# Keeping the filter's cosine products in PSUM, where DVE's sums of residue pairs read them

## The chip, the cores and the metric

The kernel runs on one core of a Trainium2 chip. The core's engines work side by side: PE (TensorE) multiplies matrices and leaves its results in PSUM, DVE (VectorE) and ACT (ScalarE) read and write both PSUM and SBUF, POOL (GpSimd) works on SBUF, and SP issues most of the transfers to and from memory. The metric is the time of one execution in microseconds (us).

## The reference

Two parts follow each other. The first multiplies x by a long convolution of x * v with a filter that a small network makes from position embeddings; the second is a feed-forward layer with a rational function in place of an activation.

```python
h_filt = (np.maximum(pos_emb @ w1, 0.0) @ w2) * np.exp(-0.01 * pos)[:, None]
u = x * v
Uf = np.fft.rfft(u, n=2 * S, axis=1)
Hf = np.fft.rfft(h_filt, n=2 * S, axis=0)
y = np.fft.irfft(Uf * Hf[None], n=2 * S, axis=1)[:, :S, :]
attn = x * y                       # (2, 12480, 128)
h = attn.reshape(-1, 128) @ w_in   # d_ff = 2048
g = (a[0] + a[1]*h + a[2]*h**2 + a[3]*h**3) / (1 + abs(b[0])*abs(h) + abs(b[1])*h**2 + 1e-6)
out = g @ w_out
```

## The kernel before

The Fourier transforms are made of matrix products with tables of cosines and sines, in two stages with a twiddle between them. A position is n = 128 * m + t; t is the residue. Stage 1 sums over m, one matmul for each channel (`s1_mm`, `L146`), and leaves K1 = 90 cosine columns and 90 sine columns per channel in a PSUM tile `cs` (two banks, 128 partitions, four channels, so 720 columns in all). The twiddle (`s1_twiddle`, `L164` and `L165`) multiplies them on DVE by a cosine and by a sine, and a complex sum makes `z`. Stage 2 multiplies over the residues on PE.

The filter takes a short cut in stage 2: the residues stand in pairs, and one half of the partitions holds one member, the other half the other. So `s1h_out` makes its sums across the halves, in four instructions of 64 partitions x 360 columns (`L551` to `L554`), which read the two twiddled tiles `ta` and `tb` from SBUF. The complex sums of the data (`s1_out`, `L170` and `L171`) are whole tiles and run on POOL.

The first part's main loop goes over g, from 0 to 34, with groups of four channels (32 groups) in a software pipeline. One iteration issues, in this order: the filter's stage 1 for group g (`L146` with `hf`, then `s1h_out` on DVE); for group g - 1 the filter's stage 2 (`L558`), its copy by ACT (`L594`) and transfer to memory, and the data's stage 1 (`L146` with `hu`, then `L164` and `L165` on DVE with `tw`, then POOL); for group g - 2 the data's stage 2 (`L181` to `L184`) and the product of the spectra (`L196` and `L197` on DVE, `L199` and `L200` on POOL); for group g - 3 the inverse stage (`L565`), ACT's copies (`L572`) and two sums on POOL (`L576`, `L577`). It ends with a piece of u = x * v on DVE (`L234`, for g below 24) or, from g = 24 on, with conversions of the second part's weights while they last.

Each engine works through its instructions in the order of the program. The PSUM tiles `cs` share four places of two banks each, with five tiles to an iteration; a new tile takes a place when the last reader of the tile that had it is done. The tags `ta` and `tb` have two places each in SBUF, which the three users of an iteration (filter, data, product) share.

The second part begins after the loop and works on its own tiles; it computes the second batch's convolution beside the feed-forward layer.

Of the kernel before, what the change touches and what calls it, by code (L numbers as in the profile page):

```python
# [9 lines left out]
F32 = mybir.dt.float32  # L10
# [3 lines left out]
ALU = mybir.AluOpType  # L14
# [6 lines left out]
N2 = 128  # L21
# [8 lines left out]
K1 = (N1 + 1) // 2  # L30
CG = 4
# [69 lines left out]
def build(ctx: ExitStack, tc, x, v, pos_emb, w1, w2, w_in, w_out, moe_a, moe_b,  # L101
          f1_d, tw_d, twh_d, dft_d, dfth_d, idft_d, idfth_d, g_d, win_d, ident_d, out):
    nc = tc.nc
# [45 lines left out]
    def pair(pool):  # L149

        t = pool.tile([N2, 2, 2, 2 * K1], F32, tag="ta", name="ta", bufs=2)
        return t, (t[:, 0], t[:, 1])

    def s1_twiddle(pool, cvt, tw, n):
        if n == 2:
            t, ab = pair(pool)
            src = cvt[:, 0, 0:4 * K1].rearrange("p (i k) -> p i k", i=2)
            nc.vector.tensor_tensor(out=t, in0=src.unsqueeze(1).to_broadcast(t.shape),
                                    in1=tw.unsqueeze(2).to_broadcast(t.shape), op=ALU.mult)
            return ab  # L160
        sh = [N2, n // 2, 2, 2 * K1]
        ta, tb = (pool.tile(sh, F32, tag=t, name=t, bufs=2) for t in ("ta", "tb"))
        src = cvt[:, 0:n // 2, 0:4 * K1].rearrange("p b (i k) -> p b i k", i=2)
        nc.vector.tensor_tensor(out=ta, in0=src, in1=tw[:, 0:1, :].unsqueeze(1).to_broadcast(sh), op=ALU.mult)  # L164
        nc.vector.tensor_tensor(out=tb, in0=src, in1=tw[:, 1:2, :].unsqueeze(1).to_broadcast(sh), op=ALU.mult)  # L165
        return ta.rearrange("p b i k -> p (b i) k"), tb.rearrange("p b i k -> p (b i) k")
# [80 lines left out]
    with ExitStack() as st:  # L247
        sp = st.enter_context(tc.tile_pool(name="sp", bufs=1))
# [4 lines left out]
        twh = sp.tile([N2, 2, 2 * K1], F32, name="twh")  # L253
# [290 lines left out]


        def s1h_out(cvt, z):
            a, bb = s1_twiddle(sp, cvt, twh, CG)
            lo, hi = slice(0, H2), slice(H2, N2)
            re, im = slice(0, K1), slice(K1, 2 * K1)
            E = nc.vector  # L550
            E.tensor_tensor(out=z[lo, 0], in0=a[lo, :, re], in1=bb[hi, :, im], op=ALU.add)  # L551
            E.tensor_tensor(out=z[hi, 0], in0=a[hi, :, im], in1=bb[lo, :, re], op=ALU.subtract)
            E.tensor_tensor(out=z[lo, 1], in0=a[lo, :, im], in1=bb[hi, :, re], op=ALU.subtract)
            E.tensor_tensor(out=z[hi, 1], in0=a[hi, :, re], in1=bb[lo, :, im], op=ALU.add)  # L554

        def s2h_mm(cvt, z):
            for i in range(2):
# [24 lines left out]
        for g in range(NG + 3):  # L582
            a = g
            if a < NG:
                zh[a] = ctile(sp, "zh", 2, CG)
                t = cvs()
                s1_mm(t, hf[a // gq], a % gq * CG, CG, MF)
                s1h_out(t, zh[a])
            a = g - 1
# [10 lines left out]
            a = g - 2  # L600
# [5 lines left out]
            a = g - 3  # L606
# [441 lines left out]
```

## Time and profile before

| | |
|---|---|
| median of 3 runs | 2523.94 us (2522.64 to 2524.48) |
| the profiled execution, its span | 2523.35 us, 2521.5 us |
| DVE, PE, ACT, POOL busy over the span | 2385.3, 2163.8, 2099.0, 544.7 us |

The span runs from the first to the last instruction that the profiler saw; the execution's own time is 1.85 us longer. Busy time says how long an engine had an instruction under way, whether or not this instruction itself made headway. [...]

### The profile page before, as it was taken

What the parts mean: (1) busy time and instruction counts of PE and PEld (TensorE: products, weight loads), DVE (VectorE), ACT (ScalarE), POOL (GpSimd) and SP (SyncE); (2) the same over time, 40 slices, a digit from 0 to 9 for tenths busy, and PEclk for the clock granted to TensorE, in tenths of its full rate; (3) what the DMA queues carried; (4) which work ended last, traced back from release to release, by engine and by line L of the source; (5) the groups of instructions that cost most, each with busy time, mean ns of one, the idle gap of its engine ahead of it and who ended that gap; (6) DMA issues with size and microseconds to landing.
All of it is one profiled execution on the core that took longest, in us unless ns stands there. A gap on an engine that the chain in (4) does not pass through costs nothing.

```text
span 2521.5 us, 33957 instructions
## 1 busy us (share of the span) xinstructions
PE 2163.8 (86%) x13344; PEld 1817.2 (72%) x13344; DVE 2385.3 (95%) x1945; ACT 2099.0 (83%) x1919; POOL 544.7 (22%) x522
## 2 busy tenths in 40 slices
PE   7888878799989998998999879887888898888887
PEld 4666666687777777787887767776776776667766
DVE  8999996999999998999999999999999999999997
ACT  5312212999999997999899999999999999999996
POOL 3466655321432143225222100000000000000000
PEclk8998998899999999999999999999999999999998
DMA  7445414622242133223222121111111111111100
GB/s 142 101 110 114 109 64 118 107 68 50 64 91 72 39 72 80 52 71 72 57 52 56 46 54 40 31 28 42 30 43 32 32 39 43 42 29 37 31 12 12
DMA packets 357825, 150.26 MB, mean 60 GB/s; under 512 B 292518, under 2 KB 339752, under 8 KB 354776
## 3 DMA queue, kind: packets, MB, share of 16 engines
q1 hardware_dynamic: 350632, 124.24, 23.4%
q10 hardware_dynamic: 7024, 23.76, 3.0%
q8 instruction: 107, 1.75, 0.3%
q14 instruction: 62, 0.51, 0.1%
HBM read 99.78 MB, written 48.17 MB: 59 GB/s over the span
## 4 chain that ended last, share of the span: by engine, by line
ACT 35%; DVE 28%; PE 24%; issue 9%; POOL 2%; DMA 1%; SPq 0%; ACTq 0%; DVEq 0%; POOLq 0%
ACT r L902 9%; ACT r L899 9%; ACT q L862 7%; PE acc L930 7%; DVE v L916 7%; ACT v L871 6%; DVE r L912 4%; DVE q L907 3%; PE cv L205 3%; PE cv L206 2%; ACT q L895 2%; DVE ta L192 2%; DVE v L881 2%; PE cs L146 1%; PE cv L146 1%
## 5 line engine op out<-in xcount | busy, mean ns | idle before, releaser
L930 PE MATMUL acc<-wout,v 128*128 128x128 f32 (+2 forms) x6656 | 833.1, 284 | 57.7 <-DVE v L916 33.7
L930 PEld LDWEIGHTS acc<-wout,v 128*128 128x128 f32 (+2 forms) x6656 | 788.7, 192 | 109.9 <-DVE v L916 52.7
L871 ACT ACTIVATE v<-h,sc 128x980 f32<-128x980 f32 (+1 forms) x416 | 640.2, 1539 | 5.5 <-PE acc L930 5.5
L862 ACT ACTIVATE q<-h 128x980 f32<-128x980 f32 (+1 forms) x416 | 582.2, 1458 | 6.6 <-PE h L854 6.6
L881 DVE SCALAR_TENSOR_TENSOR v<-v,sc,h 128x980 f32<-128x980 f32 (+1 forms) x416 | 505.3, 1215 | 64.1 <-ACT v L871 62.3
L895 ACT ACTIVATE q<-q,sc 128x1960 f32<-128x1960 f32 (+1 forms) x208 | 495.6, 2383 | 0.0
L899 ACT ACTIVATE r<-q,sc 128x1960 f32<-128x1960 f32 (+1 forms) x208 | 494.7, 2378 | 0.2 <-DVE v L916 0.2
L902 ACT ACTIVATE r<-r 128x1960 f32<-128x1960 f32 (+1 forms) x208 | 476.5, 2291 | 0.0
L907 DVE SCALAR_TENSOR_TENSOR q<-q,sc,r 128x1960 f32<-128x1960 f32 (+1 forms) x208 | 466.3, 2242 | 4.9 <-ACT r L902 1.1
L916 DVE SCALAR_TENSOR_TENSOR v<-v,sc,r 128x1960 f32<-128x1960 f32 (+1 forms) x208 | 465.4, 2238 | 0.1
L912 DVE SCALAR_TENSOR_TENSOR r<-q,r 128x1960 f32<-128x1960 f32 (+1 forms) x208 | 450.9, 2168 | 0.1
L852 PE MATMUL h<-ahi,win_l 128*128 128x490 f32 (+1 forms) x832 | 365.2, 439 | 99.5 <-DVE v L881 97.3
L853 PE MATMUL h<-alo,win_h 128*128 128x490 f32 (+1 forms) x832 | 321.5, 386 | 0.0
L854 PE MATMUL h<-ahi,win_h 128*128 128x490 f32 (+1 forms) x832 | 319.3, 384 | 0.0
L852 PEld LDWEIGHTS h<-ahi,win_l 128*128 128x128 f32 x832 | 158.9, 191 | 158.7 <-DVE v L881 133.3
L199 POOL TENSOR_TENSOR yy<-ta 128x180 f32<-128x180 f32 x64 | 117.8, 1841 | 367.5 <-DVE ta L192 367.5
L854 PEld LDWEIGHTS h<-ahi,win_h 128*128 128x128 f32 x832 | 159.2, 191 | 26.6
L853 PEld LDWEIGHTS h<-alo,win_h 128*128 128x128 f32 x832 | 159.9, 192 | 15.9 <-DVE alo L823 0.4
L798 PE MATMUL cv<-yc,gt 90*98 90x128 f32 x1004 | 130.8, 277 | 33.4 <-DVE an L804 30.7
L798 PEld LDWEIGHTS cv<-yc,gt 90*98 90x98 f32 x1004 | 114.8, 165 | 53.5 <-DVE an L804 49.7
L209 ACT ACTIVATE ys<-cv 90x512 f32<-90x512 f32 x64 | 76.9, 1202 | 71.3 <-PE cv L206 71.3
L205 PE MATMUL cv<-idft,yy 128*90 128x256 f32 x256 | 79.9, 394 | 61.4 <-DVE ta L192 36.5
(109 smaller groups left out, 2496.1 us busy)
## 6 DMA issues: line engine op xcount, KB each, us to landing
yc<-y_d SPq DMA_DIRECT2D x23, 900.0 KB
gt<-in_g_dram SPq DMA_DIRECT2D x48, 344.5 KB
h_d<-hg ACTq DMA_DIRECT2D x32, 360.0 KB
y_d<-ys ACTq DMA_DIRECT2D x16, 720.0 KB
hg<-h_d SPq DMA_DIRECT2D x64, 180.0 KB
y_d<-ys SPq DMA_DIRECT2D x16, 720.0 KB
xq<-in_x_dram SPq DMA_DIRECT2D x32, 196.0 KB
vq<-in_v_dram SPq DMA_DIRECT2D x32, 196.0 KB
```

The lines of the kernel that those rows point to most:

```text
L852: nc.tensor.matmul(out=t[:, k, 0:w], lhsT=wl, rhs=hi[:, 0:w], start=True, stop=False)
L853: nc.tensor.matmul(out=t[:, k, 0:w], lhsT=wh, rhs=lo[:, 0:w], start=False, stop=False)
L862: nc.scalar.activation(out=halves(st_q[s], i, width(s)), in_=st_h[s, i], func=AF.Abs, **({} if short else {"scale": col("b0")}))
L871: nc.scalar.activation(out=v, in_=st_h[s, i], func=AF.Square, bias=col("s"))
L881: stt(out=v, in0=v, scalar=col("k"), in1=h, op0=ALU.add, op1=ALU.mult)
L895: nc.scalar.activation(out=whole(st_q, s), in_=whole(st_q, s), func=AF.Square, bias=col("dl"))
L899: nc.scalar.activation(out=whole(st_r, s), in_=whole(st_q, s), func=AF.Ln, **({"bias": col("ka")} if short else {}))
L902: nc.scalar.activation(out=whole(st_r, s), in_=whole(st_r, s), func=AF.Exp, scale=-1.0)
L907: nc.vector.scalar_tensor_tensor(out=q, in0=q, scalar=col("ka") if short else 0.0, in1=whole(st_r, s), op0=ALU.add, op1=ALU.mult)
L912: nc.vector.scalar_tensor_tensor(out=r, in0=whole(st_q, s), scalar=2.0, in1=r, op0=ALU.subtract, op1=ALU.mult)
L916: nc.vector.scalar_tensor_tensor(out=v, in0=v, scalar=col("p0" if short else "a0"), in1=whole(st_r, s), op0=ALU.add, op1=ALU.mult)
L930: nc.tensor.matmul(out=acc[j][0:k, q // 128, :], lhsT=g[:, i, q:q + k], rhs=wout[:, f, :], start=(f == 0 and q == 0), stop=(f == NF - 1), ...
```

## The change

`s1h_out` no longer calls `s1_twiddle`. It makes the product with the sines first, to SBUF as before (`bb`, from the tag `tb`). Then it multiplies the PSUM tile by the cosines in place, and the four sums read their first input there. The tile `ta` of the filter is gone. The sums have the same shapes and the same partitions as before; the views have one dimension more, since PSUM's columns lie in two banks.

```diff
         def s1h_out(cvt, z):
-            a, bb = s1_twiddle(sp, cvt, twh, CG)
+            sh = [N2, CG // 2, 2, 2 * K1]
+            bb = sp.tile(sh, F32, tag="tb", name="tb", bufs=2)
+            a = cvt[:, 0:CG // 2, 0:4 * K1].rearrange("p b (i k) -> p b i k", i=2)
+            E = nc.vector
+            E.tensor_tensor(out=bb, in0=a, in1=twh[:, 1:2, :].unsqueeze(1).to_broadcast(sh), op=ALU.mult)
+            E.tensor_tensor(out=a, in0=a, in1=twh[:, 0:1, :].unsqueeze(1).to_broadcast(sh), op=ALU.mult)
+            z = z.rearrange("p r (b i) k -> p r b i k", i=2)
             lo, hi = slice(0, H2), slice(H2, N2)
             re, im = slice(0, K1), slice(K1, 2 * K1)
-            E = nc.vector
-            E.tensor_tensor(out=z[lo, 0], in0=a[lo, :, re], in1=bb[hi, :, im], op=ALU.add)
...
+            E.tensor_tensor(out=z[lo, 0], in0=a[lo, :, :, re], in1=bb[hi, :, :, im], op=ALU.add)
...
```

On DVE, one steady iteration of the loop before, from the filter's products to the data's (each row: line, operation, output and inputs, shape; in brackets the engines whose signals the instruction waits for):

```order
L164 TENSOR_TENSOR ta<-cs,twh 128x720 [waits DVE_49,PE_49,Pool_49]
L165 TENSOR_TENSOR tb<-cs,twh 128x720 [waits DVE_49]
L551 TENSOR_TENSOR zh<-ta,tb 64x360 [waits DVE_49]
L552 TENSOR_TENSOR zh<-ta,tb 64x360
L553 TENSOR_TENSOR zh<-ta,tb 64x360 [waits DVE_49]
L554 TENSOR_TENSOR zh<-ta,tb 64x360 [waits DVE_49]
L164 TENSOR_TENSOR ta<-cs,tw 128x720 [waits PE_49,Pool_49]
L165 TENSOR_TENSOR tb<-cs,tw 128x720
```

And the same place in the changed kernel, whose lines have numbers that are 6 higher from the sums on:

```order
L552 TENSOR_TENSOR tb<-cs,twh 128x720 [waits DVE_49,PE_49,Pool_49]
L553 TENSOR_TENSOR cs<-cs,twh 128x2x360
L557 TENSOR_TENSOR zh<-cs,tb 64x360 [waits DVE_49]
L558 TENSOR_TENSOR zh<-cs,tb 64x360
L559 TENSOR_TENSOR zh<-cs,tb 64x360
L560 TENSOR_TENSOR zh<-cs,tb 64x360
L164 TENSOR_TENSOR ta<-cs,tw 128x720 [waits PE_49]
L165 TENSOR_TENSOR tb<-cs,tw 128x720 [waits Pool_49]
```

No instruction has moved or gone: six are six, in the same place among DVE's others. The product with the cosines now comes second and writes `cs`, the sums read `cs` and `tb`, and the data's wait for POOL has moved from `ta` to `tb`.

On PE the matmuls keep their order, but the place that each `cs` tile takes has changed, and with it what is waited for. Before, from the data's stage 2 in one iteration to the start of the next (`L565` is the inverse stage, `L146` with `hf` the filter's stage 1):

```order
L181 MATMUL cs<-zu,dft 128x360 [waits PE_49,Activation_49,Pool_49]
...
L565 MATMUL cs<-idfth,yy 90x128 [waits DVE_49,PE_49,Pool_49]
L565 MATMUL cs<-idfth,yy 90x128 [waits Pool_49]
L565 MATMUL cs<-idfth,yy 90x128 x6
L146 MATMUL cs<-f_66,hf_93 128x180 [waits Activation_49]
```

In the changed kernel, over two iterations (`L571` is the inverse stage there, `L564` the filter's stage 2):

```order
L571 MATMUL cs<-idfth,yy 90x128 [waits Activation_49,Pool_49]
L571 MATMUL cs<-idfth,yy 90x128 [waits Pool_49]
L571 MATMUL cs<-idfth,yy 90x128 x6
L146 MATMUL cs<-f_66,hf_93 128x180 [waits DVE_49]
...
L564 MATMUL cs<-zh,dfth 128x360 [waits DVE_49,PE_49]
...
L571 MATMUL cs<-idfth,yy 90x128 [waits DVE_49,PE_49,Pool_49]
L571 MATMUL cs<-idfth,yy 90x128 [waits Pool_49]
L571 MATMUL cs<-idfth,yy 90x128 x6
L146 MATMUL cs<-f_66,hf_94 128x180 [waits Activation_49]
```

Before, the inverse stage took the filter's place and waited for DVE's second product, and the next filter's stage 1 waited for ACT. Now the two take turns: in one iteration the next filter's stage 1, in the other the inverse stage, waits for DVE's last sum (`L560`), while the other one waits for ACT's copy.

## Rows read from the trace of the kernel before

**Rows 1.** Busy us by stretch and engine; granted clock, DMA share, GB/s.

```profile
core 0: us, PE busy (x) PEld busy (x) DVE busy (x) ACT busy (x) POOL busy (x), PEclk, DMA share, GB/s
98.00:112.00 14.00, 14.00 (x72) 11.03 (x71) 13.68 (x20) 1.93 (x5) 6.17 (x7) 0.99 0.44 100
112.00:318.00 206.00, 179.71 (x887) 138.50 (x886) 202.81 (x222) 40.39 (x71) 140.76 (x123) 0.93 0.48 109
318.00:367.00 49.00, 37.39 (x172) 28.34 (x171) 48.12 (x66) 8.35 (x16) 26.72 (x28) 0.90 0.21 66
367.00:405.00 38.00, 34.26 (x178) 26.89 (x177) 36.33 (x42) 8.55 (x16) 25.91 (x25) 0.96 0.23 77
```

**Rows 2.** DVE's groups by shape, 60 to 460 us: busy us, mean ns.

```profile
L552 DVE TENSOR_TENSOR zh<-ta,tb 64x360 f32<-64x360 f32 x32 | 40.8, 1276 | 1.0
L551 DVE TENSOR_TENSOR zh<-ta,tb 64x360 f32<-64x360 f32 x32 | 40.8, 1275 | 1.1
...
L553 DVE TENSOR_TENSOR zh<-ta,tb 64x360 f32<-64x360 f32 x32 | 19.8, 619 | 1.0
L554 DVE TENSOR_TENSOR zh<-ta,tb 64x360 f32<-64x360 f32 x32 | 16.9, 527 | 1.0
```

**Rows 3.** Timeline, DVE, one iteration before POOL's long sums begin: start, duration.

```profile
104.04 0.89 DVE L164 TENSOR_TENSOR ta<-cs,twh 128x720 f32<-128x720 f32 x1
...
105.78 0.53 DVE L551 TENSOR_TENSOR zh<-ta,tb 64x360 f32<-64x360 f32 x1
106.34 0.53 DVE L552 TENSOR_TENSOR zh<-ta,tb 64x360 f32<-64x360 f32 x1
...
112.27 0.90 DVE L164 TENSOR_TENSOR ta<-cs,twh 128x720 f32<-128x720 f32 x1
```

**Rows 4.** Timeline, DVE and POOL, in a steady iteration.

```profile
237.31 1.26 POOL L576 TENSOR_TENSOR ys<-qt 90x512 f32<-90x512 f32 x1
...
237.34 1.63 DVE L551 TENSOR_TENSOR zh<-ta,tb 64x360 f32<-64x360 f32 x1
...
238.53 1.57 POOL L577 TENSOR_TENSOR ys<-qt 90x512 f32<-90x512 f32 x1
...
239.00 1.49 DVE L552 TENSOR_TENSOR zh<-ta,tb 64x360 f32<-64x360 f32 x1
...
243.27 0.90 DVE L196 TENSOR_TENSOR pta<-cs,hg 128x720 f32<-128x720 f32 x1
...
244.09 0.90 DVE L197 TENSOR_TENSOR ptb<-cs,hg 128x720 f32<-128x720 f32 x1
244.28 0.82 POOL L171 TENSOR_TENSOR zu<-ta,tb 128x360 f32<-128x360 f32 x1
```

**Rows 5.** Timeline, DVE: first products of iterations 24, 25, 28 and 31.

```profile
317.77 0.90 DVE L164 TENSOR_TENSOR ta<-cs,twh 128x720 f32<-128x720 f32 x1
...
332.92 0.90 DVE L164 TENSOR_TENSOR ta<-cs,twh 128x720 f32<-128x720 f32 x1
...
366.98 0.90 DVE L164 TENSOR_TENSOR ta<-cs,twh 128x720 f32<-128x720 f32 x1
...
395.44 0.91 DVE L164 TENSOR_TENSOR ta<-cs,twh 128x720 f32<-128x720 f32 x1
```

**Rows 6.** Timeline, PE, where it runs without a gap.

```profile
98.84 0.77 PE L181 MATMUL cs<-zu,dft 128*128 128x360 f32 x2
...
104.92 0.77 PE L181 MATMUL cs<-zu,dft 128*128 128x360 f32 x2
...
107.34 1.91 PE L565 MATMUL cs<-idfth,yy 128*90 128x128 f32 x16
109.09 1.39 PE L146 MATMUL cs<-f,hf 82*128 82x180 f32 x8
```

**Rows 7.** Timeline, DVE: reads of PSUM at the second part's start.

```profile
425.57 0.56 DVE L804 TENSOR_TENSOR an<-cv,xt 98x384 f32<-98x384 f32 x1 [4.45 <-PE cv L798]
428.25 0.42 DVE L804 TENSOR_TENSOR an<-cv,xt 98x256 f32<-98x256 f32 x1 [2.12 <-PE cv L798]
```

More of the change, by code (lines that the diff above doesn't have):

```diff
@@ L546, in s1h_out @@
         def s1h_out(cvt, z):
-            a, bb = s1_twiddle(sp, cvt, twh, CG)
+            sh = [N2, CG // 2, 2, 2 * K1]
[5 more added lines that the diff above has]
+            z = z.rearrange("p r (b i) k -> p r b i k", i=2)
             lo, hi = slice(0, H2), slice(H2, N2)
             re, im = slice(0, K1), slice(K1, 2 * K1)
-            E = nc.vector
-            E.tensor_tensor(out=z[lo, 0], in0=a[lo, :, re], in1=bb[hi, :, im], op=ALU.add)
-            E.tensor_tensor(out=z[hi, 0], in0=a[hi, :, im], in1=bb[lo, :, re], op=ALU.subtract)
-            E.tensor_tensor(out=z[lo, 1], in0=a[lo, :, im], in1=bb[hi, :, re], op=ALU.subtract)
-            E.tensor_tensor(out=z[hi, 1], in0=a[hi, :, re], in1=bb[lo, :, im], op=ALU.add)
+            E.tensor_tensor(out=z[lo, 0], in0=a[lo, :, :, re], in1=bb[hi, :, :, im], op=ALU.add)
+            E.tensor_tensor(out=z[hi, 0], in0=a[hi, :, :, im], in1=bb[lo, :, :, re], op=ALU.subtract)
+            E.tensor_tensor(out=z[lo, 1], in0=a[lo, :, :, im], in1=bb[hi, :, :, re], op=ALU.subtract)
+            E.tensor_tensor(out=z[hi, 1], in0=a[hi, :, :, re], in1=bb[lo, :, :, im], op=ALU.add)
         def s2h_mm(cvt, z):
```

## The prediction

> **What bounds the kernel now.** I read the busy times by stretch first [rows 1]. The change touches only the first part's loop over groups of four channels, whose last iteration ends near 405 us of the span. In it DVE is busy 202.81 of the 206 us between 112 and 318, while POOL has 140.76 and ACT 40.39. So DVE sets the pace, and a microsecond taken from DVE there is a microsecond off the end, until another engine is as full. PE, with 179.71, is the next one.
>
> Then I asked which of DVE's instructions cost more than they should. The groups by form show the four sums of `s1h_out`, all of one shape, at means of 1275, 1276, 619 and 527 ns [rows 2]. The timeline tells why. In the iteration that begins at 104.04, where POOL does not run `L576` and `L577` yet, each sum lasts 0.53 us and the next begins 0.56 us after it [rows 3]. In a steady iteration `L551` begins at 237.34, just after POOL's `L576`, ends only after it, and takes 1.63; `L552` falls on `L577` and takes 1.49 [rows 4]. Both inputs of these sums lie in SBUF. The products with one input in PSUM do not suffer: `L197` runs beside POOL's `L171` and keeps 0.90, `L196` before it has the same [rows 4]. So what is lost is mutual exclusion between POOL and a DVE instruction that reads two SBUF tensors: 1.63 + 1.49 - 2 x 0.53 = 2.06 us in an iteration.
>
> The starts of the filter's first product, `L164`, give the periods. There are 20 iterations (g = 4 to 23) from 112.27 to 317.77 [rows 3, 5], 10.275 us each, against 8.23 us from 104.04 to 112.27 [rows 3]. The difference, 2.05, is the loss just found.
>
> **The change, part by part.**
>
> *Products.* One product (with the sines, to SBUF) stays as it is. The other reads and now also writes the same PSUM tile. No row of before shows DVE writing PSUM. Lower end: no extra cost, since DVE reading PSUM costs what reading SBUF does (below). Upper end: every element needs two turns at the bank, so 0.75 us more for 720 elements (0.90 less a fixed part of some 0.15). I take 0, as the rows on reading are the nearest, and keep the upper end as a rival.
>
> *Sums.* Four per iteration, 64 x 360, now with one input in PSUM. From DVE's PSUM reads of 256 and 384 columns, 0.42 and 0.56 us [rows 7], 360 columns come to 0.53, equal to the sum from SBUF in rows 3. The step from one to the next could be shorter than 0.56: `L196` and `L197` start 0.82 apart though each takes 0.90 [rows 4], and in the same way sums would start 0.45 apart. But `L551` and `L552` have no wait between them in the order shown above, and still start 0.56 apart [rows 3]; what keeps them apart looks like the change of partition half, which stays. I take 0.56. With 0.45 the iteration would be 0.33 to 0.44 shorter, of which PE (below) would let some 0.4 through: 8 us over 20 iterations at most.
>
> [...]
>
> *Exclusion.* Gone for the sums. `L234`, which multiplies two SBUF tiles, keeps its own; it is within the 8.23. POOL's work in an iteration starts at the same instructions as before (its order does not change), and its `L577` loses the wait for the sums.
>
> *PE and the PSUM tiles.* The filter's `cs` tile is now held until the last sum, and in the order shown above one iteration's `L571`, and in the next iteration the filter's `L146`, waits for it. What PE must do in an iteration is read where it runs without a gap: 6.08 us from `L181` at 98.84 to `L181` at 104.92 (an iteration without `L565`), and 1.75 for `L565` (107.34 to 109.09): 7.83 [rows 6]. From the iteration's first product, the last sum ends after 1.74 + 3 x 0.56 + 0.53 = 3.95 us. Then `L571` and the next filter `L146` take 1.75 + 1.39 [rows 6]: 7.09, before DVE needs that tile at 8.23. So this wait is covered with 1.1 us. [...]
>
> *The sum.* 20 steady iterations x (10.275 - 8.23) = 40.9. Iteration g = 24 (317.77 to 332.92) has the same two slow sums ahead of weight work that does not change: 2.05. In g = 25 to 27 the exclusion already falls on the weight work and the sums are short: 0. From g = 28 on there is no `L234`: three periods from 366.98 to 395.44 are 9.49 each [rows 5]; DVE alone would come down to 1.74 + 4 x 0.56 + 4 x 0.82 = 7.26, but PE's 7.83 stops it, so I take 7.9: 4 x 1.59 = 6.4. Together 49.3. Off this 2 us, for a few stretches at 1.2 GHz: the mean clock was 0.93 of 2.4 GHz in the steady stretch, but 0.99 from 98 to 112, where PE had no idle time [rows 1], and with PE busy 95% of an iteration I expect the latter. So 47.3 less than the profiled execution's 2523.35 us (span 2521.5), an execution that stands 0.6 under the median of the runs: **2476 us**. As a check, the sums' excess over 0.53 is 40.8 + 40.8 + 19.8 + 16.9 - 128 x 0.53 = 50.5 us [rows 2], the most that DVE can give by this way. The second part is the same, instruction for instruction, and begins that much earlier.
>
> **The rivals.**
>
> *PE becomes the bound.* For it: 7.83 is close under 8.23; at the old mean clock it is 7.83 / 0.93 = 8.42, and with stalls at the new tile wait some 8.6. Against it: the clock in rows 1 where PE was full. Then 20 x 1.675 + 1.7 + 4 x 0.89 = 39 saved: 2484; 2497 if the period is 9.1.
>
> *The product in place runs at half rate.* 0.75 more in each iteration: 20 x 1.3 + 1.3 - 7 x 0.75 + 4 x 1.46 = 27.9 saved: 2495. Nothing in the profile speaks for or against it.
>
> *Sums from PSUM have a larger fixed cost.* Half of the fixed 0.14 us of rows 7 again would be 0.28 an iteration, 28 x 0.28 = 8 us: 2484. Against it: rows 7 and 3 together. [...]
>
> *The change doesn't do what it says.* If POOL also blocks an instruction with one SBUF input, or the lost time moves to `L234`, nothing is gained: 2523. Against it: `L196` and `L197` in rows 4.
>
> *Slower.* PSUM serves DVE at half rate in all five new accesses, the product in place and four reads by half the partitions with a change of half. That is 0.75 + 4 x 0.375 = 2.25 an iteration, above the 2.05 won; it decides from 2.05 on. Steady iterations lose 0.2 each (4 us), and the seven iterations without slow sums lose 2.25 (16): 2543. Against it: rows 7, at full rate, though with 98 partitions from the first on.
>
> **How the numbers follow.** The forecast has 0.60, PE as bound 0.17, the dearer sums 0.06, half rate in the product 0.09, no effect 0.04, slower 0.04. The range from 2470 to 2498 holds the first four and some 2 us of overlap between sums; it leaves out less than 0.2. The likeliest one's own range is 2470 to 2480. Below 0.2% (5 us) a measurement of this kernel can't tell a change from none; the first four cases are faster by more, so faster 0.92, same 0.04, slower 0.04.
>
> **What would show it.** Right: sums at 0.53 beside POOL's two long instructions, the product in place at 0.90, iterations of 8.2 to 8.3 us through the steady stretch, POOL's second long one (`L577`, 1.57 in rows 4) down to the 1.26 of the first, and DVE's first instruction of the second part (425.57 before, rows 7) near 378. Wrong: a product of 1.2 to 1.7; PE without idle time and DVE waiting for `L146` or `L184`, with a granted clock under 0.95 there; sums over 0.6; `L234` longer than before.

## The result

The changed kernel takes 2475.69 us in the median of 4 runs (2473.72 to 2477.18), the kernel before 2523.57 (4 runs, 2522.64 to 2524.48). The ratio of the two is 0.9812, with a 95% interval of 0.9801 to 0.9823 (the runs below give their ratio to the kernel before in the same way). The forecast of 2476 lies 0.3 us from the median. The profiled execution took 2475.52 us, its span is 2473.6 (2521.5 before).

### The profile page after: what moved, and what is told of

Its sections match the earlier page's. It is cut to its first block, busy times and chain, and to the rows that moved or that the text cites. A ratio compares the mean times of both kernels' runs of the same rounds, so it can differ in the third digit from the quotient of the medians.

```text
span 2473.6 us, 33923 instructions
## 1 busy us (share of the span) xinstructions
PE 2129.4 (86%) x13344; PEld 1799.1 (73%) x13344; DVE 2335.8 (94%) x1945; ACT 2098.8 (85%) x1919; POOL 534.7 (22%) x522
## 3 DMA queue, kind: packets, MB, share of 16 engines
q8 instruction: 107, 1.75, 0.3%
## 4 chain that ended last, share of the span: by engine, by line
ACT 35%; DVE 27%; PE 24%; issue 9%; POOL 2%; DMA 1%; SPq 0%; ACTq 0%; DVEq 0%; POOLq 0%
ACT r L908 9%; ACT r L905 9%; ACT q L868 7%; PE acc L936 7%; DVE v L922 7%; ACT v L877 6%; DVE r L918 4%; DVE q L913 4%; PE cv L205 3%; ACT q L901 2%; PE cv L206 2%; DVE ta L192 2%; DVE v L887 2%; PE cs L571 2%; PE cv L146 1%
## 5 line engine op out<-in xcount | busy, mean ns | idle before, releaser
L199 POOL TENSOR_TENSOR yy<-ta 128x180 f32<-128x180 f32 x64 | 119.8, 1871 | 369.5 <-DVE ta L192 369.5
```

## The profile after

First DVE's groups by shape, 60 to 460 us before [rows 2] and 60 to 420 us here, where the first part ends earlier; the columns are busy us and mean ns, then the idle time ahead.

```profile
L553 DVE TENSOR_TENSOR cs<-cs,twh 128x720 f32<-128x720 f32 x32 | 28.8, 900 | 0.0
L552 DVE TENSOR_TENSOR tb<-cs,twh 128x720 f32<-128x720 f32 x32 | 28.6, 894 | 3.9 <-POOL yy L200 2.4 <-POOL zu L171 1.5
L558 DVE TENSOR_TENSOR zh<-cs,tb 64x360 f32<-64x360 f32 x32 | 17.1, 535 | 0.4
...
L557 DVE TENSOR_TENSOR zh<-cs,tb 64x360 f32<-64x360 f32 x32 | 16.8, 525 | 1.1
```

All 128 sums are short now, 525 to 535 ns against means of 1275, 1276, 619 and 527. The product in place (`L553`) takes 900 ns, the one to SBUF 894: writing PSUM costs DVE nothing more here.

The timeline of DVE, POOL and PE in a steady iteration (start, duration, and in brackets a wait), which answers to [rows 4]:

```profile
202.67 0.89 DVE L552 TENSOR_TENSOR tb<-cs,twh 128x720 f32<-128x720 f32 x1
...
203.49 0.89 DVE L553 TENSOR_TENSOR cs<-cs,twh 128x720 f32<-128x720 f32 x1
204.38 1.27 POOL L582 TENSOR_TENSOR ys<-qt 90x512 f32<-90x512 f32 x1
204.41 0.53 DVE L557 TENSOR_TENSOR zh<-cs,tb 64x360 f32<-64x360 f32 x1
204.95 0.54 DVE L558 TENSOR_TENSOR zh<-cs,tb 64x360 f32<-64x360 f32 x1
205.50 0.53 DVE L559 TENSOR_TENSOR zh<-cs,tb 64x360 f32<-64x360 f32 x1
205.61 1.27 POOL L583 TENSOR_TENSOR ys<-qt 90x512 f32<-90x512 f32 x1
206.04 0.54 DVE L560 TENSOR_TENSOR zh<-cs,tb 64x360 f32<-64x360 f32 x1
...
206.72 1.95 PE L571 MATMUL cs<-idfth,yy 128*90 128x128 f32 x16 [0.46 <-DVE zh L560]
...
210.84 0.89 DVE L552 TENSOR_TENSOR tb<-cs,twh 128x720 f32<-128x720 f32 x1
```

The sums now lie side by side with POOL's two long instructions and neither delays the other: `L583` has the 1.27 of `L582`, where the second of the pair took 1.57 [rows 4]. PE does wait for the last sum before `L571`, but DVE has no gap for it: the next iteration begins 8.17 us after this one.

The busy times by stretch (PE, PEld, DVE, ACT, POOL; then the granted clock, which is TensorE's as a share of its full speed; DMA share, GB/s) answer to [rows 1]:

```profile
112.00:276.00 164.00, 157.20 (x872) 126.46 (x871) 161.86 (x221) 39.44 (x70) 134.31 (x123) 1.00 0.58 135
276.00:318.00 42.00, 30.61 (x151) 24.43 (x149) 41.40 (x58) 8.04 (x15) 25.36 (x25) 0.89 0.24 75
```

DVE is still the fullest engine of the loop (99%), PE is at 96%, and the granted clock of the steady stretch is 1.00. The second part begins at DVE's `L810`, 47.40 us earlier than in [rows 7]:

```profile
378.17 0.56 DVE L810 TENSOR_TENSOR an<-cv,xt 98x384 f32<-98x384 f32 x1 [4.45 <-PE cv L804]
```

From the starts of the filter's first product in both traces comes the ledger, with what the prediction gave each stretch:

| stretch | before | after | difference | forecast |
|---|---|---|---|---|
| span's start to g = 4 | 112.27 | 112.56 | +0.29 | 0 |
| g = 4 to 23 | 205.50 | 163.95 | -41.55 | -40.9 |
| g = 24 | 15.15 | 13.06 | -2.09 | -2.05 |
| g = 25 to 27 | 34.06 | 36.37 | +2.31 | 0 |
| g = 28 to 30 | 28.46 | 23.47 | -4.99 | -4.8 |
| g = 31 to the second part | 30.13 | 28.76 | -1.37 | -1.6 |
| second part | 2095.93 | 2095.43 | -0.50 | 0 |
| sum | 2521.5 | 2473.6 | -47.90 | -49.3, with 2 off: -47.3 |

## The experiments

The theory is that POOL's reads of SBUF and DVE's sums with both inputs in SBUF shut each other out, and that the change wins only by taking one input out of SBUF. The rivals are that the new order of the products, the missing tile `ta` or the new places of the PSUM tiles win something themselves, and that POOL's two instructions delay DVE in another way than by their reads.

### The order alone

The kernel before with the products in the new order, both to SBUF, and the sums reading SBUF:

```diff
         def s1h_out(cvt, z):
-            a, bb = s1_twiddle(sp, cvt, twh, CG)
+            tb, ta = (sp.tile(sh, F32, tag=t, name=t, bufs=2) for t in ("tb", "ta"))
...
+            nc.vector.tensor_tensor(out=tb, in0=src, in1=twh[:, 1:2, :].unsqueeze(1).to_broadcast(sh), op=ALU.mult)
+            nc.vector.tensor_tensor(out=ta, in0=src, in1=twh[:, 0:1, :].unsqueeze(1).to_broadcast(sh), op=ALU.mult)
```

> The kernel before with the filter's two products in the new order (sines first, cosines second), both to SBUF, and the four sums from SBUF. Theory (a sum that reads two SBUF tensors is shut out while POOL works): nothing is won, steady iterations of 10.28 us, two sums of an iteration at 1.4 to 1.65 us, 2524 us within 3. Rival (the gain came from the order of the products, the tags' places or the places of the PSUM tiles): 2476 to 2500.

Measured: 2522.91 us, ratio 1.0 (0.999 to 1.0009). The timeline of a steady iteration (start, duration) shows the same slow pair as [rows 4]:

```profile
237.46 1.27 POOL L581 TENSOR_TENSOR ys<-qt 90x512 f32<-90x512 f32 x1
237.49 1.63 DVE L556 TENSOR_TENSOR zh<-ta,tb 64x360 f32<-64x360 f32 x1
238.69 1.56 POOL L582 TENSOR_TENSOR ys<-qt 90x512 f32<-90x512 f32 x1
239.15 1.49 DVE L557 TENSOR_TENSOR zh<-ta,tb 64x360 f32<-64x360 f32 x1
240.67 0.53 DVE L558 TENSOR_TENSOR zh<-ta,tb 64x360 f32<-64x360 f32 x1
```

The order of the products wins nothing by itself. This run keeps the tile `ta`, and its PSUM tile is free after the second product, as before; the next run bears on those.

### POOL only writes

The kernel before, with POOL's two sums of the inverse stage (`L576`, `L577`) replaced by memsets of the same elements (the kernel leaves those two sums out):

```diff
-            engines[0].tensor_tensor(out=dst[:, 1:3], in0=a, in1=b, op=ALU.add)
-            engines[1].tensor_tensor(out=dst[:, 0:4:3], in0=a, in1=b, op=ALU.subtract)
+            for e, o, op in zip(engines, (dst[:, 1:3], dst[:, 0:4:3]), (ALU.add, ALU.subtract)):
+                if e is nc.gpsimd:
+                    e.memset(o, 0.0)
+                else:
+                    e.tensor_tensor(out=o, in0=a, in1=b, op=op)
```

> The kernel before with POOL's two inverse-stage sums of an iteration turned into memsets of the same elements, so that POOL writes them and reads nothing (the inverse sums are left out on POOL; the filter's sums still read two SBUF tensors). Theory, with the loss put down to POOL's reads: the filter's sums fall to 0.53 to 0.6, iterations to 8.2 to 8.35 us, and the time to 2468 to 2480 with less to wait for in the weight iterations as well. Rival (POOL's writing is enough to shut DVE out, or sums from SBUF are slow by themselves): sums of 1 us or more remain, 2500 to 2524.

Measured: 2466.66 us, ratio 0.9776 (0.9761 to 0.9791), 1.3 us below the expected range. The timeline shows DVE's sums, unchanged from before and with both inputs in SBUF, beside POOL's memsets (two in the first line, merged):

```profile
204.37 0.99 POOL L578 MEMSET ys<- 90x512 f32 x2
204.43 0.53 DVE L551 TENSOR_TENSOR zh<-ta,tb 64x360 f32<-64x360 f32 x1
204.99 0.53 DVE L552 TENSOR_TENSOR zh<-ta,tb 64x360 f32<-64x360 f32 x1
205.54 0.53 DVE L553 TENSOR_TENSOR zh<-ta,tb 64x360 f32<-64x360 f32 x1
```

With POOL writing, not reading, `L551` and `L552` take 0.53 again, and 20 iterations (112.30 to 276.65) take 8.22 us each. The two memsets are shorter than the sums they stand for (0.99 us together), but `L551` lies wholly beside them and loses nothing. So there are two ways to the same 8.2: take DVE's second input out of SBUF, or POOL's inputs away. That these sums have two SBUF inputs is harmless alone. This kernel has the old order, the tile `ta` and the old places of the PSUM tiles; as its period is within 0.02 us of the changed kernel's 8.20, those explain none of the 2.05 us that an iteration won. (Of the 9 us by which this run lies below the changed kernel, 5.9 are in iterations 24 to 27, 276.65 to 320.18 here and 276.51 to 325.94 there; the next run is about that stretch. Another 2.6 lie between g = 31 and the second part.)

So a sum of this shape takes 0.53 beside POOL's memsets with both inputs in SBUF, and 0.53 beside POOL's sums with one input in PSUM (`L557` in the changed kernel).

### The weight conversions moved

In the changed kernel, iterations 24 to 26 still take 13.1 us each. In them DVE's conversions of weights stand at the end of the iteration and fall on POOL's instructions. Here they follow right behind `s1h_out`:

```diff
+            weights = not (uw and gq * (uw[0][0] - 1) <= g)
+            if weights:
+                next(wg, None)
             a = g - 1
...
-            if uw and gq * (uw[0][0] - 1) <= g:
+            if not weights:
                 mult_u(nc.vector)
-            else:
-                next(wg, None)
```

> The changed kernel with the weight conversions of iterations 24 to 27 moved from the end of the iteration to right behind the filter's sums, where POOL waits for the data's products. Theory: the conversions run without POOL beside them, 2.3 us in place of 5.8, iterations 24 to 26 go from 13.1 to 9.6 us, and PE's long wait in iteration 27 goes too: 2462 to 2466. Rival (they meet POOL wherever they stand, or PE sets the pace there): 2472 to 2477.

Measured: 2464.95 us, ratio 0.9766 (0.9753 to 0.978). The groups of DVE from 276 to 318 us (busy us, mean ns), first of the changed kernel, then of this one:

```profile
L325 DVE TENSOR_TENSOR i<-i,i 128x256 int32<-128x256 int32 x3 | 4.4, 1483 | 0.0
L323 DVE TENSOR_SCALAR i<-raw 128x256 int32<-128x256 int32 x3 | 4.1, 1355 | 0.0
...
L320 DVE TENSOR_SCALAR i<-raw 128x256 int32<-128x256 int32 x3 | 3.1, 1032 | 0.0
```

```profile
L325 DVE TENSOR_TENSOR i<-i,i 128x256 int32<-128x256 int32 x3 | 1.2, 410 | 0.0
...
L323 DVE TENSOR_SCALAR i<-raw 128x256 int32<-128x256 int32 x3 | 0.8, 282 | 0.0
...
L320 DVE TENSOR_SCALAR i<-raw 128x256 int32<-128x256 int32 x3 | 0.8, 281 | 0.0
```

Where POOL is idle, a conversion takes 0.28 us instead of 1.03 or 1.36. `L320` and `L323` have one input, so one input alone doesn't free an instruction from the exclusion. The iterations g = 24 to 26 come down to 9.83, 9.92 and 9.95, and DVE's first instruction of the second part (378.17 in the changed kernel) to 365.97. Of these 12.2 us the median shows 10.7; the profiled execution, 2466.17 us, is the longest of its five.

The run bears on g = 27 too. With the conversions out of the way, PE's longest wait for the last sum falls. The sums of PE's waits from 100 to 350 us (us, times, longest), in the changed kernel and here:

```profile
PE cs L571 <- DVE zh L560: 19.0, 12, 6.9
```

```profile
PE cs L571 <- DVE zh L560: 10.1, 13, 1.9
```

The granted clock from 276 to 318 us rises from 0.89 to 1.00, and g = 27 takes 8.11 us (306.06 to 314.17) instead of 10.08.

### The product u = x * v moved as well

`L234`, the last DVE instruction with two SBUF inputs in the loop, put to the same place:

```diff
-            weights = not (uw and gq * (uw[0][0] - 1) <= g)
-            if weights:
+            if uw and gq * (uw[0][0] - 1) <= g:
+                mult_u(nc.vector)
+            else:
                 next(wg, None)
...
-            if not weights:
-                mult_u(nc.vector)
```

> As the run with the weight conversions moved, and DVE's piece of u is moved to the same place in the other iterations. Theory: the piece takes 1.04 in place of 1.11 to 1.16 us and POOL is not shut out by it, but the data's products come 0.88 us later and the next iteration's first product then waits for POOL's second complex sum: iterations of 8.1 to 8.3, so 2462 to 2468. Rival (that wait becomes long): 8.5 and more, over 2470.

Measured: 2476.5 us, ratio 0.9819 (0.9805 to 0.9832), 11.5 us more than with the conversions alone. The expectation failed; the rival has the time, but not its reason, for the wait that it names is short (0.15 below). The steady period is 8.755 us (113.35 to 288.44 for g = 4 to 23) against 8.195. The timeline (start, duration, wait):

```profile
202.68 1.27 POOL L582 TENSOR_TENSOR ys<-qt 90x512 f32<-90x512 f32 x1
...
203.91 1.27 POOL L583 TENSOR_TENSOR ys<-qt 90x512 f32<-90x512 f32 x1
...
204.81 1.28 DVE L234 TENSOR_TENSOR hu<-xq,vq 97x512 f32<-97x512 f32 x1
...
209.63 0.91 DVE L552 TENSOR_TENSOR tb<-cs,twh 128x720 f32<-128x720 f32 x1 [0.15 <-POOL zu L171]
```

Two things could have cost the 0.56: `L234` now falls on `L583`, and `L552` waits for POOL's `L171` to free its place of the tag `tb` (0.15).

### A third place of the tag tb

The last kernel, with a third place of `tb`, which takes that wait away (the same number is changed at the tag's other users):

```diff
-            bb = sp.tile(sh, F32, tag="tb", name="tb", bufs=2)
+            bb = sp.tile(sh, F32, tag="tb", name="tb", bufs=3)
...
```

> The kernel in which L234 stands right behind the filter's sums (2476.5), with three places instead of two for the tag tb. There each iteration took 8.76 us against 8.16 with L234 at its old place; L552 waited 0.16 for POOL's L171 to free its place of tb, and L234 took 1.25 to 1.28 instead of 1.11. If the loss has these two parts, the third place takes away only the first: the period becomes about 8.57 and the time 2472 to 2473.5, with L234 as long as before. Rival 1: the wait for the place is the whole loss: 8.2 and 2464 to 2466. Rival 2: DVE then waits for PE instead: no change, 2476.

Measured: 2473.89 us, ratio 0.9806 (0.9791 to 0.9821). The wait is gone and the period is still 8.75 (111.83 to 286.88): my reading, that the loss has two parts, was wrong. What the wait had cost, `L234` took over (timeline, start and duration):

```profile
202.65 1.27 POOL L583 TENSOR_TENSOR ys<-qt 90x512 f32<-90x512 f32 x1
...
203.30 1.52 DVE L234 TENSOR_TENSOR hu<-xq,vq 97x512 f32<-97x512 f32 x1
...
205.68 0.90 DVE L165 TENSOR_TENSOR tb<-cs,tw 128x720 f32<-128x720 f32 x1
...
206.72 0.82 POOL L170 TENSOR_TENSOR zu<-ta,tb 128x360 f32<-128x360 f32 x1 [2.80 <-DVE tb L165]
```

`L234` ends 0.90 after `L583` in this run and 0.91 in the one before, wherever it begins; it gets through only behind POOL's last read. That closes a ring: POOL's six instructions follow each other (5.94 us from `L170` at 197.98 to the end of `L583`), `L234` ends 0.90 later, `L164` and `L165` end 1.76 after it, and 0.14 after them the next `L170` begins: 8.74. The run before has the same ring, with 5.97 + 0.91 + 1.76 + 0.14 = 8.78 from `L170` at 199.21, so the wait for the place was never on it. DVE is bound there not by its own work but by the exclusion, in a ring with POOL; the next run, with the same three places and `L234` elsewhere, doesn't have it. The 2.6 us by which the median still fell are not in the period: in the traces 1.0 is there at the first product of all (83.52 against 84.56), and 2.2 at DVE's first instruction of the second part (375.70 against 377.89).

### The product u = x * v where POOL is idle

The kernel with the conversions moved, `L234` between the data's two products, and the third place of `tb`:

```diff
         nc.vector.tensor_tensor(out=ta, in0=src, in1=tw[:, 0:1, :].unsqueeze(1).to_broadcast(sh), op=ALU.mult)
+        if between is not None:
+            between()
         nc.vector.tensor_tensor(out=tb, in0=src, in1=tw[:, 1:2, :].unsqueeze(1).to_broadcast(sh), op=ALU.mult)
...
-                s1_out(sp, t, zu[a], CG)
+                s1_out(sp, t, zu[a], CG, between=None if weights else lambda: mult_u(nc.vector))
...
```

> The kernel after with the weight conversions moved (2464.95), in which also the product u = x * v (L234, two inputs in SBUF) is issued between the data's two products instead of after L197, and the tag tb has three places. In the run with the conversions moved L234 lies beside POOL's L199: it takes 1.11 us, L199 1.57 where it takes 0.95 alone. Between the data's two products POOL is idle (206.78 to 208.37 there). If DVE's loss to POOL is the sums' loss alone, L234 comes down only to its shortest, 1.03, L199 to 0.95, and as L234 began 0.94 before the next instruction already, the period stays at 8.1 to 8.2: 2462 to 2468. Rival: L234 loses much to POOL too, and alone takes some 0.7 (the rate of the other instructions for 512 columns): then DVE needs 7.8, PE's 7.83 is the bound and the time is 2457 to 2460.

Measured: 2460.38 us, ratio 0.9752 (0.9739 to 0.9765), the fastest of all kernels here. The timeline (`L236` is `L234` here, `L201` is `L199`):

```profile
204.88 1.04 DVE L236 TENSOR_TENSOR hu<-xq,vq 97x512 f32<-97x512 f32 x1
...
208.45 0.95 POOL L201 TENSOR_TENSOR yy<-pta,ptb 128x360 f32<-128x360 f32 x1
```

In the changed kernel the two stand like this:

```profile
201.72 1.11 DVE L234 TENSOR_TENSOR hu<-xq,vq 97x512 f32<-97x512 f32 x1
201.95 1.57 POOL L199 TENSOR_TENSOR yy<-pta,ptb 128x360 f32<-128x360 f32 x1
```

Apart from each other, the product takes 1.04 instead of 1.11, and POOL's instruction 0.95 instead of 1.57. So in the changed kernel it was POOL that waited, as `L234` had begun first, and DVE lost next to nothing to it. (In two of the 24 iterations `L234` fell on POOL's `L171` instead and took 1.47 and 1.48.) The rival, a much shorter `L234`, is out, though the time lies between what the two gave, and only the rows decide.

The period is 8.10 (111.03 to 272.98), 0.10 less than with the conversions alone, which makes 2 us; 0.7 of them are two iterations of 8.50 and 8.51 us there, the two in which `L234` meets `L171`, where the others take 8.16. Another 1.4 come ahead of g = 4, and 1.25 of these stand at the first product of all (83.32 against 84.57), much as in the other kernel with a third place of `tb`. DVE's first instruction of the second part comes 2.5 us earlier in the traces (363.43 against 365.97). What remains of the medians' 4.6 I have not traced.

## Why the prediction was right

*What was lost.* In the steady iterations the exclusion was the whole of it. The sums are short both when their input leaves SBUF and when POOL's inputs do, and the new order alone wins nothing.

*The price of the new operations.* Taken at 0 extra for the product in place, and measured 0.90 beside 0.89. The sums from PSUM were taken at 0.53 with a step of 0.56; measured 0.525 to 0.535, with steps of 0.54 and 0.55. The rival with dearer sums is out: 525 to 535 ns with a PSUM input stand against 527 with none [rows 2]. That the change of partition half sets the step was a guess, and no run shows it.

*The steady stretch.* 8.20 us an iteration against a forecast of 8.23, and the granted clock was 1.00 where I had left room for some of the 0.93 of before.

*PE.* It was near the bound and not the bound while `L234` was there. From g = 28 on it is: from 326 to 350 us PE is busy 24.00 of 24.00, and the three periods are 7.82 (7.9 forecast, 7.83 the sum of PE's rows).

*The wait for the PSUM place.* The prediction had it covered with 1.1 us. Once it was not, at g = 27, with a period of 10.08. An estimate from [rows 6] for a granted clock of 0.5, with 3.95 us to the last sum and then twice the 1.75 + 1.39 of `L571` and `L146`, gives 10.23. The timeline there:

```profile
315.86 0.90 DVE L552 TENSOR_TENSOR tb<-cs,twh 128x720 f32<-128x720 f32 x1
...
319.93 3.69 PE L571 MATMUL cs<-idfth,yy 128*90 128x128 f32 x16 [6.88 <-DVE zh L560]
...
323.41 2.43 PE L146 MATMUL cs<-f,hf 82*128 82x180 f32 x8
...
324.34 0.94 POOL L200 TENSOR_TENSOR yy<-pta,ptb 128x360 f32<-128x360 f32 x1
...
325.94 0.91 DVE L552 TENSOR_TENSOR tb<-cs,twh 128x720 f32<-128x720 f32 x1 [2.37 <-POOL yy L200]
```

The conversions hold DVE up, PE stands idle for 6.88 us, and then the 16 matmuls of `L571` take 3.69 instead of the 1.91 of [rows 6]; the granted clock (after the four busy times and PEld's) is 0.50:

```profile
318.40:322.00 3.60, 2.07 (x10) 2.10 (x11) 3.54 (x6) 0.00 (x0) 0.32 (x1) 0.50 0.22 85
```

`L552` waits 2.37 us. The view names POOL's `L200`, but that ended at 325.28; `L146` ended at 325.84, just before `L552` began. In the kernel before, PE was as slow in the inverse stage (3.59, with a granted clock of 0.51 from 361.15 to 364.57), but started it earlier:

```profile
359.29 0.90 DVE L164 TENSOR_TENSOR ta<-cs,twh 128x720 f32<-128x720 f32 x1
...
361.15 3.59 PE L565 MATMUL cs<-idfth,yy 128*90 128x128 f32 x16 [4.88 <-DVE tb L165]
...
364.57 1.39 PE L146 MATMUL cs<-f,hf 82*128 82x180 f32 x8
```

There the inverse stage began 1.86 us after the iteration's first product, in the changed kernel 4.07 after it: 2.2 us later, because the place is free only after the last sum. The filter's `L146` behind it then took 2.43 us, 1.0 more than the 1.39 of before, as the granted clock was still low (0.56 from 323.4 to 325.8 us). Of these 3.3 us 1.0 was covered: in the kernel before, `L146` had ended at 365.96 and DVE's next product began at 366.98 [rows 5]. What is left is the 2.4 us that g = 27 lost (10.08 against 7.69). The low clock in the inverse stage alone had cost the kernel before nothing; the later start and the slow `L146` cost the changed one together. With the conversions moved, PE's long wait, the low clock and the stall went together, so that run does not part the place from the clock.

*The sum.* The steady stretch won 0.65 more than forecast, g = 25 to 27 lost 2.3 where I had set down 0, and 2 us had been taken off for stretches at a low clock without saying where. No run shows the clocks in GHz that the prediction names there; the traces give shares of full speed, 0.50 and 0.56 at g = 27 and 1.00 in the steady stretch. The place and the low clock did meet in that one iteration, and cost about as much, 2.4 us. That the total is right to 0.3 us is still luck: the terms miss by up to 2.3 us, and what they missed largely cancels against those 2.

## What to carry to other kernels

Where a DVE instruction takes more than twice its usual time in some iterations only, look at what POOL reads in that time: in these traces two inputs in SBUF on DVE and POOL's reads shut each other out, and the one that started first made the other wait (`L576` before `L551` in [rows 4], 1.63 us instead of 0.53; `L234` before `L199` above, 1.57 instead of 0.95). Leave one factor in PSUM, if DVE makes it there anyway, or put the instruction where POOL is idle; moving it by a little can close a ring with POOL that costs more than the exclusion did (0.56 us an iteration for `L234`). And a PSUM tile that is kept longer is a wait for PE: here it cost nothing in the steady iterations, and 2.4 us in the one where other work made DVE late and PE's granted clock was 0.50 to 0.56.

## What the runs showed of the hardware

- DVE's product in place in PSUM, 128 partitions and 720 columns, takes 900 ns, as to SBUF (894).
- One input is no safe conduct: DVE's `tensor_scalar` of 128x256 int32 takes 1.03 to 1.36 us beside POOL's sums and 0.28 with POOL idle.
- An excluded DVE instruction ended the same time behind POOL's read in two runs (`L234`: 0.90 and 0.91 us after `L583`), though it had begun 0.37 before that end in one and 0.62 in the other.
- With the shorter period PE's idle time in the steady stretch shrank to 6.8 of 164 us, from 26.3 of 206 [rows 1], and the granted clock there rose from 0.93 to 1.00. With `L234` behind the filter's sums (a period of 8.755) the clock from 112 to 276 us was 1.00 too, with 12.5 of 164 us idle.
